# Attention followed by a feed-forward layer: the later q, k, v loads issued by GpSimd instead of SyncE

## The chip, the core and the metric

The program runs on one core of one Trainium2 chip. Its engines work at the same time, each through its own list of instructions in order: TensorE (PE; matmuls, with their weight loads shown apart as PEld), VectorE (DVE), ScalarE (ACT), GpSimd (POOL) and SyncE (SP, which here issues transfers and computes nothing). They meet through semaphores. Sixteen DMA engines move data between the main memory (HBM) and the core's memory (SBUF); a transfer is started by an instruction on the queue of SP, ACT or POOL. TensorE writes its sums to PSUM banks, which VectorE and ScalarE empty. The metric is the time of one execution in microseconds, as the device has it; the medians of several runs are compared.

## The reference

A linear attention with cosine weights, then a two-layer network over all tokens (batch 8, 8 heads, 576 tokens, 64 per head; 512 to 2048 to 512):

```python
def phi(x, c, s):
    r = np.maximum(x, 0.0)
    return np.concatenate([r * c, r * s], axis=-1)
q_p = phi(q, cos_w, sin_w)
k_p = phi(k, cos_w, sin_w)
kv = np.einsum('bhsf,bhsd->bhfd', k_p, v)
z = np.sum(k_p, axis=2)
num = np.einsum('bhsf,bhfd->bhsd', q_p, kv)
den = np.einsum('bhsf,bhf->bhs', q_p, z)[..., None] + 1e-06
attn = num / den
...
h = x @ w_in
g = np.maximum(0.01 * h, h)
return (g @ w_out).astype(np.float32)
```

`x` is the attention's output with the heads of a token side by side, 4608 x 512. Inputs and output are fp32; the kernel computes in fp16 with fp32 sums.

## The kernel before, in words

The kernel goes through the 8 batches b = 0 to 7, and a ninth group, g = 8, takes the last 64 tokens of all batches together. A batch's first 512 tokens are its main part, the other 64 its tail.

For each batch, three fp32 main tiles of 1 MB arrive (q, k, v; `load_main`, L88 to L96), laid out as 128 partitions x 8 heads x 4 tokens x 64, so that each partition takes eight runs of 1 KB from HBM: 1024 runs a tile. The tails of k and v (`load_kvtail`, L98 to L104) are 64 x 4 runs of 256 B in each of two transfers; the tails of q of all batches come late, in eight transfers of 64 x 8 runs of 256 B (`load_qtail`, L106 to L113).

Main tiles share three buffers ("stage", L84 to L86, with two of the w_out tiles and the q tails) and the k and v tails share three others ("kvtail"). A load can start when the last reader of its buffer is done.

The readers are on VectorE and ScalarE. `q_part` and `k_part` take one quarter of a tile at a time and write relu(x) times the cosine or sine to fp16 (L240 on VectorE, L238 on ScalarE); `v_main` converts v to fp16 (L248 on VectorE, L246 on ScalarE). TensorE then forms kv (L289, L298), q is transposed by a DMA from SBUF to SBUF (L346), TensorE forms the numerators and denominators (`num`, L380), VectorE divides (L391 to L396), the result xs is transposed by DMA again (L357), and the two layers follow: `p1` (L785) for the first, `p2` (L890) for the second. From batch 2 on both use Strassen-like sums of quarter matrices, so that VectorE and ScalarE have sums (L251, L254), copies (L795, L805, L908) and the leaky relu (L798, L812) to do beside the loads' conversions. Results leave by `o_store` (L915).

Everything is put in an order written out by hand: each step has a position in one list (`put(position, function, ...)`), the list is sorted by position, and the instructions come out in this order on each engine. The positions of the loads of batches 3 and up are the entries `'load'` of the table `AT`; with them SP's order from batch 3 on is q, k, k tails, v, v tails (batch 3), v, v tails, k, k tails, q (batch 4), then q, k, k tails, v, v tails for each of 5, 6 and 7, with the DMA transposes and the stores in between. Batches 0 to 2 and the weights are loaded by explicit calls earlier. All of these loads are issued by SP in the kernel before. GpSimd makes constants at the start and converts some of w_in and v (L248); its last work is at 46.58 us.

Of the kernel before, what the change touches and what calls it, by code (L numbers as in the profile page):

```python
# [13 lines left out]
P = 128  # L14
# [4 lines left out]
def kernel(  # L19
# [14 lines left out]
    nc = tc.nc  # L34
# [49 lines left out]
    def staged(shape, name, soon=False):  # L84
        p, tag = (early, "early") if soon else (stage, "stage")
        return p.tile(shape, dt.float32, name=name, tag=tag)  # L86

    def load_main(nm, src, b, parts=(0, 1), soon=False):  # L88

        if parts[0] == 0:  # L90
            st[nm, b] = staged([P, H, J, D], f"{nm}st", soon)
        lo, hi = 4 * parts[0], 4 * parts[-1] + 4
        nc.sync.dma_start(
            st[nm, b][:, lo:hi],
            src[b, lo:hi, 0:MAIN, :].rearrange("h (p j) d -> p h j d", j=J),
        )  # L96

    def load_kvtail(nm, src, b):  # L98

        t = kvtail.tile([P, H // 2, D], dt.float32, name=f"{nm}tl", tag="kvtail")  # L100
        v4 = src[b, :, MAIN:S, :].rearrange("(c o) p d -> o p c d", o=2)
        for o in range(2):
            nc.sync.dma_start(t[o:P:2], v4[o])
        st[nm + "t", b] = t  # L104

    def load_qtail(i):  # L106
        if i == 0:
            st["qt"] = staged([P, J, H, D], "qtl")
        for o in range(2):
            nc.sync.dma_start(  # L110
                st["qt"][o * TAIL : (o + 1) * TAIL, i],
                q[2 * i + o, :, MAIN:S, :].rearrange("h p d -> p h d"),
            )  # L113

    def load_k(b):
        load_main("k", k, b)
        load_kvtail("k", k, b)

    def load_v(b):
        load_main("v", v, b)  # L120
        load_kvtail("v", v, b)
# [20 lines left out]
    def load_w2(i):  # L142
        t = staged([P, 4, DM], "w2st", i > 1)
        nc.sync.dma_start(t, w2v[i])
        st["w2", i] = t

    load_main("q", q, 0, (0,))
    load_main("q", q, 0, (1,))
    load_main("k", k, 0, (0,))
    load_main("v", v, 0, (0,))  # L150
    load_kvtail("k", k, 0)
    load_kvtail("v", v, 0)
    load_main("k", k, 0, (1,))
# [943 lines left out]
    for b in range(2, NG):  # L1097
        at_, eng, s0 = AT[min(b, 5)], ENG[min(b, 5)], top[b] if b > 3 else 0
        if b < B:
            for n, pos_ in enumerate(at_.get("load", ())):  # L1100
                put(s0 + pos_, loads, b, n)
            put(s0 + min(at_["kc"] + at_["ks"]) - 0.01, kp_tiles, b)
            for j in range(J + 1):
                put(s0 + at_["kc"][j], k_part, b, j, 0, eng["kc"][j])
                put(s0 + at_["ks"][j], k_part, b, j, 1, eng["ks"][j])
            for n in range(3):
                put(s0 + at_["v"][n], v_part, b, n, eng["v"][n])
            put(s0 + at_["kv"][0], kv_all, b)
        else:
            for j in range(J):  # L1110
                put(s0 - 100 + 3 * j, load_qtail, j)
        for j in range(J):
            put(s0 + at_["qc"][j], q_part, b, j, 0, eng["qc"][j])
            put(s0 + at_["qs"][j], q_part, b, j, 1, eng["qs"][j])
            put(s0 + at_["qt"][j], q_transpose_dma, b, j)
            put(s0 + at_["num"][j], num, b, j)
            put(s0 + at_["xt"][j], x_transpose if b == 2 else x_transpose_dma, b, j)
            put(s0 + at_["xs"][j], x_sums, b, j + 1)
# [33 lines left out]
```

## Time and profile before

| | us |
|---|---|
| median of 3 runs | 272.52 |
| lowest, highest | 271.55, 272.92 |
| the profiled execution, its own time | 273.88 |
| its span, first to last instruction | 272.0 |
| TensorE, VectorE, ScalarE, GpSimd busy in the span | 264.6, 201.0, 200.7, 10.1 |

The page of the profile also shows the DMA queues (share is that of the time of 16 engines):

```profile
q1 hardware_dynamic: 86816, 56.37, 78.1%
q8 instruction: 21, 0.34, 0.5%
```

q1 is SP's queue with its packets, megabytes and share.

How to read the rows. A row of the timeline has the start and the length in us, the engine, the line of the kernel, the operation, what it writes `<-` what it reads, and the shapes; `xN` means N of a kind merged, and brackets hold the idle time before it and what ended that. SPq is SP's queue: the length of a `DMA_DIRECT2D` row there is the time in which SP issues the transfer, not the transfer's own. "To landing" is the time from the start of the issue to the arrival. The chain of waits goes back from the last instruction, at each step to what released it. A row of a sum by stretch has the stretch, its length, and for each engine the busy time with the number of instructions (PE, PEld, DVE, ACT, POOL), the granted clock of TensorE, the DMA engines' share and GB/s. Tile names: `qst`, `kst`, `vst` are the main tiles of q, k and v, `ktl`, `vtl`, `qtl` the tails.

### The profile page before, as it was taken

To read this page: it belongs to the slowest core of one execution; us is meant where nothing else is said; L and a number is where in the kernel's file an instruction comes from. 1 tells how busy PE (TensorE), PEld (TensorE's weight loads), DVE (VectorE), ACT (ScalarE), POOL (GpSimd) and SP (SyncE) were. 2 spreads that over 40 slices of the span, in tenths; PEclk is the share of its full clock that TensorE was granted. 3 is DMA by queue.
4 is the path that set the end of the run, shared out by engine and by line. 5 is a ranking of instruction groups with operands and counts; after the bars stand their busy time and mean duration, and the time that the engine had idled before them with its cause. 6 is when DMAs were issued, how large, how long until landed. Compare 5 with 4: busy or idle time off the path is not lost.

```text
span 272.0 us, 6597 instructions
## 1 busy us (share of the span) xinstructions
PE 264.6 (97%) x2660; PEld 226.8 (83%) x2660; DVE 201.0 (74%) x444; ACT 200.7 (74%) x331; POOL 10.1 (4%) x21
## 2 busy tenths in 40 slices
PE   8999999999999999999999999999999999999994
PEld 5876555665898979889999999999999989999983
DVE  5774589797986797899779696978577757645652
ACT  6756556696878898798899789978966657766621
POOL 1055101000000000000000000000000000000000
PEclk9999999999999999999999999999999999999999
DMA  6999989998999959997999699967274312200314
GB/s 228 318 374 413 398 291 361 368 267 254 309 208 342 175 178 264 312 172 228 259 280 161 183 276 275 181 212 155 62 149 144 61 41 96 80 0 2 154 39 118
DMA packets 87150, 57.05 MB, mean 210 GB/s; under 512 B 56656, under 2 KB 82256, under 8 KB 86608
## 3 DMA queue, kind: packets, MB, share of 16 engines
q1 hardware_dynamic: 86816, 56.37, 78.1%
q8 instruction: 21, 0.34, 0.5%
q10 hardware_dynamic: 304, 0.26, 0.4%
q14 instruction: 9, 0.07, 0.1%
HBM read 36.70 MB, written 9.44 MB: 170 GB/s over the span
## 4 chain that ended last, share of the span: by engine, by line
PE 69%; DMA 3%; DVE 2%; ACT 2%; issue 1%; ACTq 0%; DVEq 0%
PE ps_o L890 31%; PE ps_h L785 27%; PE ps_h L495 3%; DMA qst<-in_q_dram 3%; PE ps_h L890 3%; PE ps_num L380 2%; PE ps_kv L289 2%; DVE gs L254 1%; PE ps_kv L298 0%; ACT g L798 0%; PE ps_xt L445 0%; ACT g L812 0%; DVE xw L254 0%; ACT qp L238 0%; DVE xs L396 0%
## 5 line engine op out<-in xcount | busy, mean ns | idle before, releaser
L890 PEld LDWEIGHTS <-g 128*128 128x128 f16 x640 | 62.5, 98 | 7.3 <-DVE g L251 0.2
L251 DVE TENSOR_TENSOR u<-ps_h,u 128x512 f32<-128x512 f32 x52 | 35.8, 688 | 25.7 <-PE ps_h L785 22.9
L890 PE MATMUL ps_o<-w,g 128*128 128x256 f16 x352 | 51.2, 273 | 0.0
L785 PEld LDWEIGHTS <-w 128*128 128x128 f16 x416 | 44.5, 114 | 1.2
L785 PE MATMUL ps_h<-xT,w 128*128 128x256 f16 x288 | 43.3, 273 | 0.0
L785 PEld LDWEIGHTS <-wa 128*128 128x128 f16 x312 | 34.0, 113 | 2.0 <-DVE xw L254 0.9
L812 ACT ACTIVATE g<-u 128x1024 f16<-128x1024 f32 x26 | 27.5, 1058 | 10.9 <-DVE u L251 10.8
L798 ACT ACTIVATE g<-ps_h 128x512 f16<-128x512 f32 x52 | 31.2, 602 | 5.7 <-PE ps_h L785 5.7
L805 ACT COPY u<-ps_h 128x512 f32<-128x512 f32 x52 | 30.4, 585 | 5.4 <-PE ps_h L785 5.4
L890 PE MATMUL ps_o<-wb,g 128*128 128x256 f16 x232 | 33.5, 273 | 0.0
L785 PE MATMUL ps_h<-xw,wa 128*128 128x256 f16 x208 | 31.3, 273 | 0.6 <-DVE xw L254 0.6
L890 PEld LDWEIGHTS <-gs 128*128 128x128 f16 x256 | 24.9, 98 | 2.9
L908 ACT COPY ob<-ps_o 128x512 f32<-128x512 f32 (+1 forms) x32 | 17.9, 561 | 9.2 <-PE ps_o L890 9.0
L495 PE MATMUL ps_h<-xT,w 128*128 128x512 f16 (+1 forms) x104 | 24.7, 363 | 0.0
L396 DVE TENSOR_TENSOR xs<-ps_num,rden 128x512 f16<-128x512 f32 x28 | 19.4, 691 | 1.0
L890 PE MATMUL ps_o<-w,gs 128*128 128x256 f16 x120 | 17.8, 273 | 0.0
L251 DVE TENSOR_TENSOR ob<-ps_o,ob 128x512 f32<-128x512 f32 (+1 forms) x22 | 14.9, 675 | 3.7 <-ACT ob L908 1.4
L890 PE MATMUL ps_o<-wb,gs 128*128 128x256 f16 x120 | 17.5, 273 | 0.0
L254 DVE TENSOR_TENSOR gs<-g 128x1024 f16<-128x1024 f16 x16 | 11.0, 689 | 8.3 <-ACT g L812 8.1
L795 ACT COPY ps_h<-ps_h 128x512 f32<-128x512 f32 x26 | 14.9, 572 | 2.0 <-PE ps_h L785 1.1
L785 PE MATMUL ps_h<-xw,w 128*128 128x256 f16 x104 | 15.6, 273 | 0.0
L785 PE MATMUL ps_h<-xT,wa 128*128 128x256 f16 x104 | 15.6, 273 | 0.0
(113 smaller groups left out, 408.6 us busy)
## 6 DMA issues: line engine op xcount, KB each, us to landing
qst<-in_q_dram SPq DMA_DIRECT2D x7, 1024.0 KB, 7.0
out_dram<-ob SPq DMA_DIRECT2D x14, 512.0 KB, 2.8
kst<-in_k_dram SPq DMA_DIRECT2D x6, 1024.0 KB, 8.3
vst<-in_v_dram SPq DMA_DIRECT2D x6, 1024.0 KB, 7.1
w1st<-in_moe_w_in_dram SPq DMA_DIRECT2D x8, 512.0 KB, 9.4
w2st<-in_moe_w_out_dram SPq DMA_DIRECT2D x4, 1024.0 KB, 13.8
kst<-in_k_dram SPq DMA_DIRECT2D x4, 512.0 KB, 7.5
vst<-in_v_dram SPq DMA_DIRECT2D x4, 512.0 KB, 7.8
```

Of the source, the lines that this page charges most:

```text
L251: nc.vector.tensor_tensor(out=o, in0=a, in1=b, op=ALU.add)
L254: nc.vector.tensor_tensor(out=o, in0=a, in1=b, op=ALU.subtract)
L289: nc.tensor.matmul(ps[:, n * NE : (n + 1) * NE - 1], lhsT=kpm[:, h, j, :], rhs=vmain[:, h, j, 0 : NE - 1], start=(n == 0 and j == 0), stop ...
L396: nc.vector.tensor_tensor(out=xs, in0=ps[:, :, 0 : 4 * NE].rearrange("p a (b e) -> p a b e", e=NE)[:, :, :, 0:D], in1=rden.rearrange("p (a ...
L495: nc.tensor.matmul(ps[:, lo:hi], lhsT=w1[m // 4][c // 2][:, c % 2, m % 4 : 512 : 4], rhs=st["xT", g][:, c, lo:hi], start=(c == 0 and lo == 0),
L785: nc.tensor.matmul(bank[:, p], lhsT=w(c), rhs=st["xb", g][n][:, c], start=(fresh and p == 0 and c == 0), stop=(c == 1), skip_group_check=True,
L795: nc.scalar.copy(bank1[bj], bank1[bi])
L798: nc.scalar.activation(st["g" + nm, g][:, 2 * t : 2 * t + 2], bank1[bi], AF.Lrelu)
L805: nc.scalar.copy(st["u", g, t][:, n], bank1[bi])
L812: nc.scalar.activation(st["gt", g][:, :, 1, 2 * t : 2 * t + 2], st["u", g, t], AF.Lrelu)
L890: nc.tensor.matmul(bank, lhsT=st[G2[n], g][:, m, pair * P : (pair + 1) * P], rhs=W2[n](m), start=(fresh and m == 0), stop=(m == NH - 1), s ...
L908: nc.scalar.copy(o_at(g, half_, col, pair), bank_of(bi, pair, pair is None))
```

## The change

The loads of q, k and v of batches 3 to 7 (the fourth batch on) are issued on GpSimd's queue, and so are the tails of q. The transfers' shapes, their types, their order among themselves and their places in the list stay; so do the loads of batches 0 to 2 and of the weights, the DMA transposes and the stores, all on SP.

```diff
+    def loader(b):
+        return nc.sync if b < 3 else nc.gpsimd
+
     def load_main(nm, src, b, parts=(0, 1), soon=False):
 
         if parts[0] == 0:
             st[nm, b] = staged([P, H, J, D], f"{nm}st", soon)
         lo, hi = 4 * parts[0], 4 * parts[-1] + 4
-        nc.sync.dma_start(
+        loader(b).dma_start(
             st[nm, b][:, lo:hi],
             src[b, lo:hi, 0:MAIN, :].rearrange("h (p j) d -> p h j d", j=J),
         )
@@
         for o in range(2):
-            nc.sync.dma_start(t[o:P:2], v4[o])
+            loader(b).dma_start(t[o:P:2], v4[o])
         st[nm + "t", b] = t
 
     def load_qtail(i):
         if i == 0:
             st["qt"] = staged([P, J, H, D], "qtl")
         for o in range(2):
-            nc.sync.dma_start(
+            nc.gpsimd.dma_start(
                 st["qt"][o * TAIL : (o + 1) * TAIL, i],
                 q[2 * i + o, :, MAIN:S, :].rearrange("h p d -> p h d"),
             )
```

## The prediction

> **What bounds the kernel now.** I read the page's engine table and its chain first, to see who sets the end.
>
> ```profile
> PE 264.6 (97%) x2660; PEld 226.8 (83%) x2660; DVE 201.0 (74%) x444; ACT 200.7 (74%) x331; POOL 10.1 (4%) x21
> PE 69%; DMA 3%; DVE 2%; ACT 2%; issue 1%; ACTq 0%; DVEq 0%
> ```
>
> TensorE is busy 97% of the span, and the chain runs through it. A modelled busy time can hide slack, so next comes the sum by stretch (columns: length, then the busy time of each engine with its instructions).
>
> ```profile
> 62.00:98.00 36.00, 35.12 (x354) 29.02 (x351) 29.05 (x68) 29.27 (x49) 0.00 (x0) 1.00 1.10 261
> 98.00:190.00 92.00, 91.83 (x1003) 85.67 (x1004) 76.53 (x164) 79.83 (x137) 0.00 (x0) 1.00 0.97 223
> 190.00:262.00 72.00, 72.00 (x719) 67.06 (x717) 46.52 (x86) 48.87 (x82) 0.00 (x0) 1.00 0.29 77
> ```
>
> From 62 us on, where the moved loads are issued and used, TensorE is idle 0.88 + 0.17 + 0 = 1.05 us before the tail, at full granted clock. So there is at most 1.05 us to win, 0.4%. There is much more to lose, because VectorE and ScalarE, which empty TensorE's banks, are themselves busy 81 to 87% of 62 to 190 us, and each works in its own order: one of them that waits for a load holds up everything behind it. VectorE's waits for loads in 62 to 190 us are these (total, times, longest):
>
> ```profile
> DVE qp L240 <- DMA qst<-in_q_dram: 0.7, 1, 0.7
> DVE kpm L240 <- DMA kst<-in_k_dram: 0.6, 1, 0.6
> ```
>
> They are short, but they show that some loads land just when they are needed. The chain of waits passes through one, batch 4's q:
>
> ```profile
> 84.31 8.12 DMA qst<-in_q_dram
> ...
> 98.17 0.63 PE ps_h L785 x4
> ```
>
> That load sets when VectorE and ScalarE go on, and the piece that they hand to TensorE at 98.17 is late by it. A microsecond more on this load is a microsecond more on the end.
>
> **The change part by part.** Every load of batches 3 to 7 leaves SyncE's queue for GpSimd's: 15 main loads of 1 MB (1024 pieces of 1 KB), 20 tails of 64 KB (256 pieces of 256 B) and 8 q tails of 128 KB (512 pieces). Bytes, tiles and readers stay. Three things follow.
>
> *First, what SyncE no longer holds back.* SyncE's queue around batches 3 and 4 (start, length):
>
> ```profile
> 61.74 0.54 SPq L93 DMA_DIRECT2D qst<-in_q_dram  x1
> 62.33 0.56 SPq L93 DMA_DIRECT2D kst<-in_k_dram  x1
> 66.09 0.55 SPq L93 DMA_DIRECT2D vst<-in_v_dram  x1
> 71.12 6.82 SPq L346 DMA_TRANSPOSE qpT<-qp  x4
> 77.98 0.59 SPq L93 DMA_DIRECT2D vst<-in_v_dram  x1
> 80.05 0.54 SPq L93 DMA_DIRECT2D kst<-in_k_dram  x1
> 80.63 3.58 SPq L103 DMA_DIRECT2D ktl<-in_k_dram  x2
> 84.31 0.55 SPq L93 DMA_DIRECT2D qst<-in_q_dram  x1
> ```
>
> Loads stand behind transposes here (v of batch 4 behind 6.82 us of them). On GpSimd a load waits only for its staging buffer and for the loads ahead of it. The buffers are three; the last reads that free them, and the first reads of what lands, are on VectorE
>
> ```profile
> 57.78 0.69 DVE L248 CAST vmain<-vst 128x1024 f16<-128x1024 f32 x1
> 71.47 0.48 DVE L240 TENSOR_SCALAR kpm<-kst,sin_t 128x512 f16<-128x512 f32 x1
> 74.38 0.48 DVE L240 TENSOR_SCALAR qp<-qst,sin_t 128x512 f16<-128x512 f32 x1
> 92.53 0.49 DVE L240 TENSOR_SCALAR qp<-qst,cos_t 128x512 f16<-128x512 f32 x1 [0.75 <-DMA qst<-in_q_dram]
> ```
>
> and on ScalarE
>
> ```profile
> 67.79 0.72 ACT L238 ACTIVATE qp<-qst,cos_t 128x512 f16<-128x512 f32 x1
> 77.95 1.05 ACT L246 CAST vmain<-vst 128x1024 f16<-128x1024 f32 x1
> 78.90 0.73 ACT L238 ACTIVATE kpm<-kst,sin_t 128x512 f16<-128x512 f32 x1
> 89.32 0.73 ACT L238 ACTIVATE kpm<-kst,cos_t 128x512 f16<-128x512 f32 x1 [0.33 <-DMA kst<-in_k_dram]
> ```
>
> So batch 3's first buffer is free at 58.5 (end of the 57.78 row) instead of an issue at 61.74, a lead of 3.2 us; batch 4's v can go at 74.9 instead of 77.98 (3.1); its k at 79.6 instead of 80.05 (0.4); its q's buffer is free at 79.0, so q follows k's tails directly. What SyncE gains (transposes and stores no longer queue behind loads) I price at nothing: TensorE waits 0.17 us in 98 to 190 us, so nothing earlier can be used. The transposes also no longer share one queue with the loads: they may land sooner and the loads later. I price that at nothing too, within 1 us either way.
>
> *Second, what GpSimd's own issue costs.* No run here has a load on GpSimd; the engine's last work is this:
>
> ```profile
> 24.74 1.34 POOL L248 CAST w<-w1st 128x1024 f16<-128x1024 f32 x1 [0.28 <-DMA w1st<-in_moe_w_in_dram]
> 46.58 1.04 POOL L248 CAST vmain<-vst 128x1024 f16<-128x1024 f32 x1 [18.15 <-DMA vst<-in_v_dram]
> ```
>
> After 47.6 it is idle, so nothing else is queued behind its waits. Near bound: it issues like SyncE, 0.55 us a main load. Far bound: it works out the 1024 pieces one after the other; its casts take 1.04 us for 1024 elements a partition, 1.0 ns a step, and with eight steps a piece a main load takes 8.3 us. I choose three steps (source, target, length): 3.1 us a main load, 0.8 a tail, 1.6 a q tail, an estimate, nearer SyncE's row than the far end because the pieces are regular. [...]
>
> Now the ends of issue, with 3.1, 0.8 and these buffer times. Batch 3: q 61.6, k 64.7, two tails 66.3, v 69.4, tails 71.0. SyncE ended them at 62.28, 62.89 and 66.64: q is 0.7 earlier, k 1.8 later, v 2.8 later. The first reads are at 67.79 (q), 71.47 (k) and 77.95 (v), and the page gives k's landing:
>
> ```profile
> kst<-in_k_dram SPq DMA_DIRECT2D x6, 1024.0 KB, 8.3
> ```
>
> 8.3 us from an issue at 62.33 puts k at 70.6, with 0.9 us of slack, so k comes some 0.9 late; v, at 66.09 + 8.3 = 74.4, has 3.5 us and isn't late. Batch 4: v 78.0, tails 79.6, k 82.7, tails 84.3, q 87.4. SyncE ended k at 80.59 and q at 84.86. So k is 2.1 later and q 2.5 later, and both had no slack at all (the reads at 89.32 and 92.53 waited for them). These overlap on the same two engines, so the stage pays the larger: **2.5 us**.
>
> Later batches, in the same way (SyncE, then ScalarE, then landing times of q in 95 to 272 us):
>
> ```profile
> 124.95 0.37 SPq L93 DMA_DIRECT2D qst<-in_q_dram  x1
> ...
> 151.66 0.37 SPq L93 DMA_DIRECT2D qst<-in_q_dram  x1
> 156.06 0.90 SPq L93 DMA_DIRECT2D kst<-in_k_dram  x1
> ```
> ```profile
> 150.58 1.06 ACT L246 CAST vmain<-vst 128x1024 f16<-128x1024 f32 x1
> 160.55 0.71 ACT L238 ACTIVATE qp<-qst,sin_t 128x512 f16<-128x512 f32 x1
> ```
> ```profile
> DMA to landing us min/median/max: 5.6/6.2/7.0
> ```
>
> k waits behind other work on SyncE until 156.06 while its buffer is free at 151.6; on GpSimd q ends at 154.7 and k at 157.8, against 156.96: 0.8 later. q had no lead (issued when its buffer was free) and 160.55 − 151.66 − 7.0 = 1.9 us of slack; it ends 3.1 − 0.4 = 2.7 later, so 0.8 late. With batch 3's k (0.9) that is 1.7 us of lateness at places where other work waits on the two engines; I count a third, **0.5 us**. The q tails, 8 × 1.6 = 13 us from 178 us, come before a stretch in which TensorE has 72.00 of 72.00 us of work; nothing.
>
> *Third, the port.* GpSimd and VectorE get in each other's way in this trace:
>
> ```profile
> 25.22 1.41 DVE L254 TENSOR_TENSOR wa<-wa,w 128x1024 f16<-128x1024 f16 x1
> 26.66 0.69 DVE L254 TENSOR_TENSOR wa<-w,wa 128x1024 f16<-128x1024 f16 x1
> ```
>
> VectorE's subtraction took 1.41 us beside GpSimd's cast of 24.74 to 26.08 and ended 0.55 after it, the same form took 0.69 us alone; the cast took 1.34 instead of 1.04. Whether issuing loads does this is not shown: from nothing to the whole of the rival below. I take **0.5 us**.
>
> Sum: 2.5 + 0.5 + 0.5 = 3.5 us. On the profiled execution (273.88 us, of which 272.0 are its span) that is 277.4; that execution lies 1.36 us over the median of the runs, so against 272.52 the forecast is **276.0 us**. Bounds: at 0.55 us an issue every lead is a gain and the most is −1.05 (271.5); at five steps (5.1 and 1.3) all six main loads and eight tails run back to back and batch 4's q ends at 58.5 + 6 × 5.1 + 8 × 1.3 = 99.5, 14.6 later than 84.86: 287. At four steps (4.1 and 1.0) it is 58.5 + 24.6 + 8 = 91.1, 6.2 later: 279 to 280; at two, q is level and k 1.1 later: 274.
>
> **The rivals.** *Cheap issue.* GpSimd issues in about 1 us. Then only leads remain: batch 4's q ends at 82 (k from 79.6, then two tails and q at 0.25 and 1), 2.8 us earlier, and the 0.75 us wait goes, while 98 to 262 us cannot shrink. Gain 0 to 1.05: 271.5 to 272.8, no slower than before. For it: nothing else is on GpSimd. Against: 1024 pieces in each load.
>
> *The port is held.* While GpSimd writes a load's pieces VectorE's conversions from the staged tiles (L240 and L248) cannot start.
>
> ```profile
> 62.00:190.00 128.00, 22.01 (x50) 1.00 1.01 234
> 62.00:190.00 128.00, 4.11 (x6) 0.00 (x0) 1.00 1.01 234
> ```
>
> These are 26.1 us of 128 on VectorE, 56 operations. 15 main loads × 3.1 us that each block one such operation half the time for half an issue make 15 × 0.5 × 1.5 = 11 us of stalls; VectorE has 128 − 105.6 = 22 us idle there, half of the stalls come out at TensorE: 6 more, 282. Held the other way, GpSimd writes 20% longer (26.1 of 128): 0.6 us a load, 277.5. [...] The rows at 24.74 and 25.22 agree that the two block each other (1.41 for 0.69 us); for loads no run shows it.
>
> *Slow issue.* At 8.3 us a main load and 2.1 a tail a batch costs 3 × 8.3 + 4 × 2.1 = 33 us of GpSimd, more than the 26.7 us between two q loads (124.95 to 151.66 in the queue); then GpSimd is the bound: 5 × 33 = 167 us from 58.5 end at 225:
>
> ```profile
> 174.32 0.69 DVE L248 CAST vmain<-vst 128x1024 f16<-128x1024 f32 x1
> ```
>
> Here VectorE reads batch 7's v, at 174: some 50 us late, 320. At five steps it is the 287 of above. For it: the pieces are short. Against: 8.3 us is eight steps a piece.
>
> **How the numbers follow.** Forecast case (two to four steps, 273.9 to 280): 0.42. Cheap issue: 0.30, of which 0.05 for a median under 271.2 (the spread of the runs helps) and 0.25 for no change. Port held: 0.14 (280 to 286). Slow issue: 0.14 (284 up). Range: 271.4 leaves out 0.05 below; above I cut at 288, which leaves out most of the slow case, 0.11. The forecast's own range is 273.9 to 280. A measurement here tells about 0.5% (1.4 us) from no change: faster 0.05, same 0.25, slower 0.70.
>
> **What would show it.** Right: load issues on GpSimd of 2 to 4 us each; waits of VectorE or ScalarE for qst or kst near 89 to 97 us of 2 us or more; TensorE's busy time in 62 to 98 us short by about 3.5; few waits after 100. Cheap issue: batch 4's q landing before 92.4 and no such wait. Port held: L240 rows longer than 0.48 us, or 22 us of L240 in 62 to 190 grown. Slow issue: v and k later from batch to batch, and waits for vst. I am wrong if TensorE's idle time after 62 us stays near 1 us, or if it grows where no load is waited for.

## The result and the profile after

The changed kernel takes **290.62 us** (median of four runs, 285.52 to 292.98) against 272.05 us (median of four, 271.55 to 272.92) for the kernel before on the same chip. The ratio is 1.057, with a 95% interval of 1.051 to 1.063; it leaves out runs more than 1.5% above the fastest of their kernel, two of the four here, and so lies below the quotient of the medians, 1.068. The profiled execution is the longest of the four, 292.98 us, with a span of 291.2 us: 19.2 us more than the span of 272.0 before. The forecast was 276.0 us with a range up to 288.0: the direction was right, and the loss is four to five times the one forecast (3.5 us), by the ratio or by the medians.

In the changed kernel all lines from L93 on stand three lower (L93 is L96, L346 is L349, L380 is L383, L785 is L788). First the page of the profile after: busy time, the chain of waits by engine, and the DMA queues (packets, MB, share of 16 engines).

```profile
PE 268.5 (92%) x2660; PEld 227.7 (78%) x2660; DVE 202.3 (69%) x444; ACT 200.4 (69%) x331; POOL 42.6 (15%) x64
...
q1 hardware_dynamic: 61552, 38.28, 50.9%
q0 software_dynamic: 5104, 18.09, 22.8%
...
PE 71%; DMA 20%; SPq 3%; issue 2%; DVE 2%; ACT 1%; POOL 0%; DVEq 0%; POOLq 0%
```

The chain of waits now has DMA for 20% of the span, where it had 3%. Of the bytes, 18.09 MB went to a second queue, in packets of 4096 B for the most part (4416 of the 5104 in the trace); SyncE's queue is left with the rest. Now the sum by stretch, over the same stretches as in the prediction (busy us with instructions of PE, PEld, DVE, ACT, POOL, then TensorE's granted clock, DMA share, GB/s).

```profile
62.00:98.00 36.00, 29.09 (x274) 22.56 (x274) 21.29 (x51) 20.68 (x34) 7.41 (x11) 0.86 0.78 222
98.00:190.00 92.00, 83.79 (x873) 75.73 (x872) 67.92 (x147) 71.52 (x123) 15.87 (x21) 0.96 0.93 201
190.00:262.00 72.00, 72.00 (x754) 67.38 (x753) 51.91 (x102) 54.11 (x90) 5.67 (x8) 1.00 0.47 108
```

TensorE is idle 6.91 + 8.21 + 0 = 15.12 us in 62 to 262, where it was idle 1.05: 14.07 us more. The clock has fallen too. The same view cut finer shows where both happen:

```profile
66.00:73.00 7.00, 0.55 (x6) 0.26 (x6) 0.67 (x2) 2.34 (x4) 0.00 (x0) 0.69 1.06 320
73.00:78.00 5.00, 5.00 (x24) 2.61 (x25) 3.45 (x8) 0.95 (x2) 0.00 (x0) 0.50 0.20 73
78.00:98.00 20.00, 20.00 (x211) 17.49 (x210) 14.76 (x35) 15.52 (x28) 5.26 (x7) 0.98 0.80 222
98.00:120.00 22.00, 21.73 (x229) 19.35 (x228) 19.14 (x42) 19.20 (x34) 5.43 (x7) 1.00 0.90 163
120.00:127.00 7.00, 1.05 (x13) 0.71 (x12) 0.83 (x2) 1.12 (x3) 0.00 (x0) 0.73 0.97 219
127.00:130.00 3.00, 3.00 (x12) 1.52 (x11) 1.72 (x5) 0.41 (x1) 0.00 (x0) 0.50 1.14 317
...
180.00:188.00 8.00, 6.01 (x63) 5.15 (x61) 4.10 (x9) 7.97 (x14) 2.13 (x3) 1.00 1.21 238
```

There are two long stalls, at 66 (6.45 us idle) and at 120 (5.95), and a short one at 180 (1.99). Between them TensorE is full. Behind each long stall it works for some microseconds at a clock of 0.50, where a 128x512 matmul of L498 takes 616 to 634 ns instead of 379. By the clock a busy 5.00 us there does the work of 2.5, an estimate: 2.5 + 0.4 + 1.5 = 4.4 us more are lost in 73 to 78, 78 to 98 and 127 to 130. Idle time and half clock together make 14.07 + 4.4 = 18.5 of the 19.2 us.

What TensorE's matmuls wait for (total, times, longest):

```profile
PE ps_num L383 <- DMA qpT<-qp: 13.1, 3, 6.5
```

It is not a load. It is `qpT`, q's transpose by a DMA from SBUF to SBUF, which SyncE still issues as before. Its issue is not late; its landing is. For the last two transposes of batch 2's q, issued between 58.4 and 61, after and then before, the tile's view gives the issue (duration in ns, first and last start) and the time to landing:

```profile
L349 SPq DMA_TRANSPOSE qpT<-qp x2: 1247/1254/1260, 58.4 to 59.7; - x2
...
DMA to landing us min/median/max: 2.9/8.1/13.2
```
```profile
L346 SPq DMA_TRANSPOSE qpT<-qp x2: 1247/1247/1247, 59.0 to 60.4; - x2
...
DMA to landing us min/median/max: 2.8/2.8/2.8
```

The one issued at 59.7 took 13.2 us instead of 2.8 and landed at 72.9, where the first stall ends. In the kernel before, the same transpose landed at 63.2 and TensorE used it at 66.98, a reserve of 3.8 us. What changed beside it is on GpSimd's timeline:

```profile
58.88 1.03 POOL L96 DMA_DIRECT2D qst<-in_q_dram  x1 [12.37 <-DVE kpt L243]
59.91 0.89 POOL L96 DMA_DIRECT2D kst<-in_k_dram  x1
60.79 1.24 POOL L106 DMA_DIRECT2D ktl<-in_k_dram  x2
62.02 0.89 POOL L96 DMA_DIRECT2D vst<-in_v_dram  x1
62.91 1.24 POOL L106 DMA_DIRECT2D vtl<-in_v_dram  x2
```

GpSimd issues a main load in 0.89 us, so that all 3 MB of batch 3 are under way by 64.2. In the kernel before they stood behind the two transposes in one queue. Now they are in another queue, beside the second of them. The DMA queues in 67 to 72, after and then before:

```profile
q0 software_dynamic: 410, 1.52, 92.5%
q1 hardware_dynamic: 412, 0.10, 10.5%
```
```profile
q1 hardware_dynamic: 2270, 1.87, 110.0%
```

410 packets of the one queue and 412 of the other: in these 5 us the counts are those of two queues that are served in turn, one packet each. But a packet of the loads is 4096 B and one of the transpose 256 B, so the loads get 92.5% of the engines' time and the transpose 10.5%. That the engines serve the two in turn is read from these counts alone (220 to 225 in 67 to 70, 190 to 187 in 70 to 72).

Equal turns are not the whole delay. In 61 to 65 the loads already run and the same transpose hardly moves:

```profile
q0 software_dynamic: 172, 0.70, 83.5%
q1 hardware_dynamic: 78, 0.02, 3.9%
```

Of its 1024 packets (256 KB in pieces of 256 B) most go only after 65: in 65 to 67 the counts are 119 of the loads' queue and 540 of the other. Why the first 4 us belong to the loads and the next 2 to the transpose is not shown. The second stall also has a part that turns do not explain: in 119 to 122 both queues almost stand still, with 35 and 20 packets and 45 GB/s. That standstill stays open.

### The profile page after: what moved, and what is told of

Same layout as the page of the kernel before. It is cut to its first block, busy times and chain, and to the rows that moved or that the text cites. A ratio compares the mean times of both kernels' runs of the same rounds, so it can differ in the third digit from the quotient of the medians.

```text
span 291.2 us, 6626 instructions
## 1 busy us (share of the span) xinstructions
PE 268.5 (92%) x2660; PEld 227.7 (78%) x2660; DVE 202.3 (69%) x444; ACT 200.4 (69%) x331; POOL 42.6 (15%) x64
## 3 DMA queue, kind: packets, MB, share of 16 engines
q0 software_dynamic: 5104, 18.09, 22.8%
## 4 chain that ended last, share of the span: by engine, by line
PE 71%; DMA 20%; SPq 3%; issue 2%; DVE 2%; ACT 1%; POOL 0%; DVEq 0%; POOLq 0%
PE ps_o L893 25%; PE ps_h L788 22%; DMA qpT<-qp 12%; PE ps_h L498 6%; PE ps_h L462 5%; PE ps_o L478 5%; DMA qst<-in_q_dram 4%; PE ps_h L893 3%; DMA w1st<-in_moe_w_in_dram 3%; PE ps_num L383 2%; SPq L96 2%; PE ps_kv L292 1%; DMA xT<-xs 1%; SPq L106 1%; PE ps_qt L368 1%
## 5 line engine op out<-in xcount | busy, mean ns | idle before, releaser
L893 PEld LDWEIGHTS <-g 128*128 128x128 f16 x640 | 63.4, 99 | 8.5 <-issue 0.8
L893 PE MATMUL ps_o<-w,g 128*128 128x256 f16 x352 | 52.0, 276 | 0.0
L788 PEld LDWEIGHTS <-w 128*128 128x128 f16 x416 | 44.5, 114 | 2.6 <-issue 1.3
L788 PE MATMUL ps_h<-xT,w 128*128 128x256 f16 x288 | 43.3, 273 | 0.0
L788 PEld LDWEIGHTS <-wa 128*128 128x128 f16 x312 | 34.0, 113 | 1.9 <-DVE xw L257 0.6
L815 ACT ACTIVATE g<-u 128x1024 f16<-128x1024 f32 x26 | 27.5, 1057 | 10.9 <-DVE u L254 10.8
L893 PE MATMUL ps_o<-wb,g 128*128 128x256 f16 x232 | 34.3, 277 | 0.0
L788 PE MATMUL ps_h<-xw,wa 128*128 128x256 f16 x208 | 31.3, 273 | 0.3 <-DVE xw L257 0.3
L498 PE MATMUL ps_h<-xT,w 128*128 128x512 f16 (+1 forms) x104 | 27.3, 392 | 0.0
L383 PE MATMUL ps_num<-kv,qpT 128*128 128x65 f16 (+1 forms) x256 | 12.2, 198 | 13.6 <-DMA qpT<-qp 13.1
L383 PEld LDWEIGHTS <-qpT 128*128 128x128 f16 (+1 forms) x256 | 10.6, 103 | 17.1 <-DMA qpT<-qp 13.9
L394 DVE TENSOR_SCALAR den<-ps_num 128x8 f32<-128x8 f32 x28 | 4.6, 164 | 20.0 <-PE ps_num L383 19.8
## 6 DMA issues: line engine op xcount, KB each, us to landing
kst<-in_k_dram POOLq DMA_DIRECT2D x5, 1024.0 KB, 12.8
```

What stands on the lines that cost most here:

```text
L383: nc.tensor.matmul(ps[lo:hi, h // 4, (h % 4) * NE : (h % 4 + 1) * NE - 1], lhsT=qpT[:, h, lo:hi], rhs=kv[b][:, h, 0 : NE - 1],)
L498: nc.tensor.matmul(ps[:, lo:hi], lhsT=w1[m // 4][c // 2][:, c % 2, m % 4 : 512 : 4], rhs=st["xT", g][:, c, lo:hi], start=(c == 0 and lo == 0),
L788: nc.tensor.matmul(bank[:, p], lhsT=w(c), rhs=st["xb", g][n][:, c], start=(fresh and p == 0 and c == 0), stop=(c == 1), skip_group_check=True,
L815: nc.scalar.activation(st["gt", g][:, :, 1, 2 * t : 2 * t + 2], st["u", g, t], AF.Lrelu)
L893: nc.tensor.matmul(bank, lhsT=st[G2[n], g][:, m, pair * P : (pair + 1) * P], rhs=W2[n](m), start=(fresh and m == 0), stop=(m == NH - 1), s ...
```

## The experiments

**Theory A:** GpSimd's queue stands beside SyncE's; while its loads run, the DMA transposes get only every other packet, TensorE waits for them, and then runs at half clock. **Rival B:** it is the early start of the loads that hurts, on any queue, ScalarE's as well. **Rival C:** GpSimd's issue, or what it holds up on VectorE (the prediction's "port"), is what costs. **Rival D:** any 2 MB at that moment hold a transpose up, in the same queue too. Ratios are to the kernel before, run on the same chip.

**Batch 3 alone, by GpSimd** (`only3_pool`), to see one stall by itself:

```diff
-        return nc.sync if b < 3 else nc.gpsimd
+        return nc.gpsimd if b == 3 else nc.sync
@@ load_qtail
-            nc.gpsimd.dma_start(
+            nc.sync.dma_start(
```

> Only batch 3's loads are on GpSimd, all others on SyncE as before. Theory A (two queues share each DMA engine packet by packet, 4096 B of a load against 256 B of a transpose, so the transpose of batch 2's q that TensorE needs next lands only when the loads are nearly done): the first stall comes back alone, TensorE idle some 6.5 us near 66 us and some 2.5 us of half clock behind it; 272 + 9 = 281 us, no wait for qpT later. Rival C (GpSimd's issuing as such, or the port it shares with VectorE): the loss goes by the number of loads, 3 of 15, so 272 + 19/5 = 276 us without a wait of TensorE for qpT.

Measured: 282.08 us (280.63 to 282.42), ratio 1.035 (1.030 to 1.040). Sum by stretch, then the wait:

```profile
66.00:74.00 8.00, 1.16 (x11) 0.56 (x10) 1.09 (x2) 2.88 (x5) 0.00 (x0) 0.78 1.06 303
74.00:78.00 4.00, 4.00 (x23) 1.90 (x21) 3.45 (x8) 0.30 (x1) 0.00 (x0) 0.58 0.22 79
...
98.00:190.00 92.00, 91.72 (x993) 84.98 (x991) 76.36 (x164) 80.44 (x140) 0.00 (x0) 1.00 0.92 221
```
```profile
PE ps_num L383 <- DMA qpT<-qp: 6.8, 1, 6.8
```

One stall, at the same place, with the same half clock behind it, and from 98 us on only 0.28 us idle. Seven of the 43 loads cost 9.7 of the 18.6 us by the medians, 3.5 of 5.7% by the ratios.

**All but batch 3 by GpSimd** (`from4_pool`), the other half:

```diff
-        return nc.sync if b < 3 else nc.gpsimd
+        return nc.sync if b < 4 else nc.gpsimd
```

> Batch 3's loads are back on SyncE, batches 4 to 7 and the q tails stay on GpSimd. Theory A: the stall near 66 us and its half clock are gone, the later ones (near 120 and 180 us in the changed kernel) stay, some 10 us earlier: 272 + 10 = 280 to 284 us. Rival C: four fifths of the loss, 272 + 15 = 287 us.

Measured: 283.23 us, but the four runs go from 277.40 to 288.27; ratio, formed as above, 1.021 (1.014 to 1.029). In the profiled execution, one of the short ones, the first stall is gone, and `qpT` is waited for once:

```profile
PE ps_num L383 <- DMA qpT<-qp: 2.5, 1, 2.5
```
```profile
111.00:114.00 3.00, 0.53 (x8) 0.25 (x6) 0.72 (x2) 0.95 (x2) 0.00 (x0) 0.92 1.08 296
114.00:118.00 4.00, 4.00 (x27) 2.54 (x25) 1.72 (x5) 0.99 (x2) 0.00 (x0) 0.63 1.12 298
```

By medians the two halves lose 9.7 and 10.9 us, 20.6 together, against 18.6 for the whole; by the ratios 3.5 and 2.1%, against 5.7%. The spread, 10.9 us, leaves the size of this half open, but not its kind.

**The same loads, kept behind the transpose** (`only3_pool_gated`): as `only3_pool`, but GpSimd first copies a column of that transpose's result, so that its loads start when it has landed.

```diff
+    gate = const.tile([P, 1], dt.float16, name="gate")
     def loads(b, which):
+        if b == 3 and which == 0:
+            nc.gpsimd.tensor_copy(gate, st["qpT", 2, 3][:, 0, 0:1])
```

> The same as the kernel with batch 3 alone on GpSimd, but GpSimd first copies one column of batch 2's last transposed q tile, so that its loads start only when that transpose has landed (about 61.2 us instead of 58.9). Theory A: nothing is left to collide with, the stall near 66 us is gone, 272 to 274 us. Rival C: the same loads are issued by the same engine, so the loss of the ungated kernel stays.

Measured: 278.13 us (277.29 to 279.60), ratio 1.021 (1.015 to 1.026). The transpose lands in 3.1 us and TensorE waits for none. But the gate opens at 65.89 and the first load is issued at 66.56, 5.4 us later than expected, and now the load is late. The first reader's wait, then TensorE's:

```profile
ACT qp L241 <- DMA qst<-in_q_dram: 4.5, 2, 3.8
```
```profile
PE ps_o L893 <- ACT xT L449: 3.6, 1, 3.6
```

So the stall on the transpose goes when the loads don't run beside it, as theory A has it. Of the time, 4.0 of the 9.7 us come back: the gate makes a stall of 3.6 us of its own. In the profiled execution, the longest of the four, another 2.4 us are lost in 0 to 30 us, ahead of batch 3's loads (TensorE idle 4.32 us there instead of 1.95); why is not shown.

**ScalarE's queue instead of GpSimd's** (`only3_act`, and `act3_early` with the loads' positions moved forward so that they start with the transpose). Both return `nc.scalar` for batch 3, and the second also has:

```diff
-    3: {'load': (20.5, 24.0, 32.0)
+    3: {'load': (15.0, 15.1, 15.2)
```

> Batch 3's loads on ScalarE's queue: a queue of its own beside SyncE's, but with packets of 1024 B as SyncE's loads have. Theory A: against 1024 B the transpose gets one part in five of the bytes instead of one in seventeen; if loads and transpose meet, the transpose lands 2 to 4 us late instead of 10, and the time is 273 to 277 us. Rival B (the loads merely start 3 us earlier and take the DMA engines, whatever the queue): as bad as on GpSimd, 281 us.

> Batch 3's loads on ScalarE's queue, and earlier in the list, so that they start at about 58 to 60 us as they did on GpSimd and meet batch 2's last transpose. Theory A: load packets of 1024 B, so the transpose's 64 packets an engine let only 1 MB pass (2.7 us): it lands before 67 us; ScalarE's own waits for the buffers cost 1 to 3 us; 273 to 276 us. Rival B (the early start is what hurts, whatever the queue): the transpose lands near 72 us as on GpSimd, TensorE waits some 6 us for qpT, 281 us.

`only3_act`: 273.10 us (272.04 to 277.94), ratio 1.0035 (0.9996 to 1.0073). Its first load was issued at 60.20, when the transposes were all but done (the last landed at 61.47), so it says little on B. `act3_early`: 282.47 us (281.77 to 282.87), ratio 1.038 (1.035 to 1.041), as bad as GpSimd, but for another reason. Its waits, then ScalarE's timeline:

```profile
PE ps_num L383 <- ACT kv L315: 7.8, 1, 7.8
```
```profile
60.18 2.71 ACTq L106 DMA_DIRECT2D ktl<-in_k_dram  x2
62.98 0.77 ACTq L96 DMA_DIRECT2D vst<-in_v_dram  x1
63.80 4.71 ACTq L106 DMA_DIRECT2D vtl<-in_v_dram  x2
68.55 0.59 ACT L315 CAST kv<-ps_kv 128x520 f16<-128x520 f32 x1 [8.05 <-issue]
```

ScalarE spends 60 to 68.5 issuing loads, and the kv that TensorE needs waits behind them. The transpose issued at 59.69 landed 9.8 us later, less than the 13.2 beside GpSimd, more than the 7.3 or less that was expected. The time says nothing on B here, since ScalarE's own stall covers it.

**Only the q loads by GpSimd** (`q_only_pool`): the five main loads of q, 1 MB at a time.

```diff
+        (nc.gpsimd if nm == "q" and b > 2 else nc.sync).dma_start(
```

> Only the five q main loads of batches 3 to 7 are on GpSimd, k, v and all tails on SyncE. Theory A: a transpose is 64 packets on each DMA engine and lets at most as many load packets pass; one main load is 16 packets of 4096 B an engine, so a transpose is held up by at most the time of 1 MB, 2.7 us, less than its slack of some 4 us near 66 us: no wait of TensorE for qpT, 272 to 275 us. Rival C: the loss goes by the number of main loads, a third of 19 us, 278 us.

Measured: 277.55 us (276.22 to 278.81), ratio 1.019 (1.013 to 1.024). This is the number that rival C gave, so the sizes of A were wrong here. But the waits aren't C's:

```profile
PE ps_num L383 <- DMA qpT<-qp: 1.2, 2, 0.9
```
```profile
ACT qp L241 <- DMA qst<-in_q_dram: 4.7, 2, 3.3
```

The transpose of 60.47 landed 8.0 us later, and in the last two batches q itself is late: GpSimd issued it in 0.88 us each time, so the issue is not slow, but beside SyncE's traffic, which is now k, v and the transposes, it took 8.9 and 11.3 us to land, where the kernel before has 6.2 and 7.0. I had counted the packets as if only one side paid. (The 2.7 us for 1 MB was an estimate; the kernel before moves 375 GB/s in 67 to 72, which makes 2.8.)

**The cause by itself** (`extra_pool`, `extra_act`, `extra_sync`). To take the edit, the late loads and the issuing engine's own work out of it, these add to the kernel before two loads of 1 MB that nothing reads, at 199 us, where TensorE has some reserve. The first two put them on GpSimd's and on ScalarE's queue, behind a copy of a column of `xs`; the third on SyncE's own queue, right behind the same two transposes (here without the copy, with `nc.sync`, at the place of the second transpose).

```diff
+    gate = const.tile([P, 1], dt.float16, name="gate")
+    def extra():
+        nc.gpsimd.tensor_copy(gate, st["xs", 7, 4 - 1][:, 0, 0:1])
+        for n in range(2):
+            nc.gpsimd.dma_start(
+                staged([P, H, J, D], f"spare{n}"),
+                (k, v)[n][3, :, 0:MAIN, :].rearrange("h (p j) d -> p h j d", j=J),
+            )
+    put(top[7] - 6.89, extra)
```

> The kernel before with two more loads of 1 MB that nothing reads, issued by GpSimd when batch 7's last xs tile is written (about 197 us), where the DMA engines are nearly idle, just ahead of two transposes of qp that landed 3.9 and 3.5 us after their issue in the kernel before and were read 7 us later. Theory A: 32 load packets of 4096 B an engine pass during the first transpose's 64: both transposes land some 5 us later than before, 8 to 9.5 us after issue; the time is unchanged, 272 to 273 us, because nothing needs them sooner. Rival B and C: a transpose already under way is not held up by loads on another queue: 4 to 5 us.

> The same two loads on ScalarE's queue with the same start. Theory A: 128 packets of 1024 B an engine; the first transpose's 64 packets let 64 pass, 1 MB: it lands 2.7 us later than before, 6 to 7 us after issue, the second some 5 us later, 8 to 9 us; 272 to 274 us. If the size of the packets does not matter, both are as late as with GpSimd's loads.

> The kernel before with two loads of 1 MB that nothing reads, issued by SyncE right behind the two transposes of about 199 us, so in the same queue as they. Theory A (it is the second queue that holds the transposes up; one queue serves in order): the two transposes land as in the kernel before, 3 to 5 us after their issue, although 2 MB are issued within 2 us of them; what is behind the loads lands later, up to 7 us. Rival D (any 2 MB at that time holds them up, whatever queue): they land 9 to 13 us after their issue, as beside the same loads on another queue. Time by A 272 to 274, by D 275 to 276.

The time from issue to landing of the two transposes at about 199 us (201 and 203 in the run with ScalarE's queue), as the tile's view has it (the lower, the middle, the higher of the two): in the kernel before, with the loads on GpSimd's queue, on ScalarE's, and on SyncE's.

```profile
DMA to landing us min/median/max: 3.5/3.7/3.9
```
```profile
DMA to landing us min/median/max: 12.8/13.0/13.3
```
```profile
DMA to landing us min/median/max: 9.4/9.7/10.0
```
```profile
DMA to landing us min/median/max: 4.2/4.3/4.4
```

The same 2 MB make the transposes take 3.5 times as long from GpSimd's queue, 2.6 times from ScalarE's, and 1.2 times from their own. The times are 275.99 us (two runs), ratio 1.015 (1.009 to 1.020); 275.02 (two runs), 1.011 (1.004 to 1.018); 272.78 (nine), 1.0001 (0.998 to 1.002). The first two do not measure the extra loads alone: TensorE waits for a `qpT` only in the first, 0.9 us, and in the profiled executions it is idle 4.31 and 5.69 us in 0 to 190 us, ahead of the extra loads, where the kernel before has 3.35; with ScalarE's loads it is not idle at all in 190 to 262. So it is the landings that test the theory here.

Rival D falls for the kernel with one queue: there the loads went out at 201.6, when the transposes of 197.9 and 199.3 were some 2 us or less from landing, and cost nothing. What 2 MB that move at the very same time in that queue would do, the run doesn't show. What of rival B stands is that ScalarE's queue does it too. Its loads have packets of 1024 B, GpSimd's of 4096 B, which fits the smaller delay; but the two queues may differ in more, so that the packet size decides is argued and not shown. Turns by packets show here too, with ScalarE's loads in 207 to 210:

```profile
q10 hardware_dynamic: 746, 0.76, 82.8%
q1 hardware_dynamic: 741, 0.19, 31.7%
```

(q10 is ScalarE's queue.) And as in the first stall the loads go ahead before that: 817 packets to 14 in 203 to 206. Theory A had the sign of all three and the sizes of `extra_sync`; for the other two its sizes were too small, most of all beside GpSimd.

**Why too little: the loads where nothing else runs** (`extra_quiet`): the same two loads by GpSimd, behind a tile of the last group.

```diff
+        nc.gpsimd.tensor_copy(gate, st["g11", 8][:, 0, 0:1])
...
+    put(top[8] + 20, extra)
```

> The kernel before with the same two unread loads of 1 MB by GpSimd, but behind the gate of a late tile of the last group, where no transpose is in flight. Beside transposes the pair landed 12.5 us after the second issue. If the two queues only alternate, the 2 MB alone take about 6 us (the rate of the main loads on SyncE's queue) and the pair lands 6 to 8 us after its first issue: mixing slows both sides. If GpSimd's packets are slow by themselves: 10 to 13 us here too. Time: 272 to 274.

The two loads, from issue to landing: alone (issued at 237.2 and 238.2), then beside the transposes (198.8 and 199.8).

```profile
DMA to landing us min/median/max: 6.6/7.6/8.5
```
```profile
DMA to landing us min/median/max: 8.9/10.7/12.5
```

Alone the pair is done 8.51 + 1.03 = 9.5 us after its first issue, beside the transposes 13.6: between the two answers that were expected, so both sides pay. The packets themselves last longer when mixed. Means over all packets of the trace, in ns:

```
                          4096 B of GpSimd    256 B of transposes
loads alone  225 to 250        193                  20
before       198 to 205         -                   26
mixed        198 to 213        256                  36
```

The single run took 274.96 us, with TensorE idle after 100 us no longer than before; one run has no interval, and the 2.7 us above the median before are not explained.

**Only the tails by GpSimd** (`tails_pool`): 20 of the 43 moved instructions, but 1.3 of the 18 MB.

```diff
-            loader(b).dma_start(t[o:P:2], v4[o])
+            (nc.gpsimd if b > 2 else nc.sync).dma_start(t[o:P:2], v4[o])
```

> Only the 20 tails of k and v of batches 3 to 7 (64 KB each) are issued by GpSimd; main loads and q tails are SyncE's as in the kernel before. Theory A (packets of a second queue hold the transposes up, in proportion to their bytes): a pair of tails is 128 KB against 2 MB of a pair of main loads, so a transpose beside them is held up by well under 1 us and TensorE never waits: 271.5 to 272.8, no change. Rival C (GpSimd's issue or the port is what costs): 20 of the 43 instructions moved are here, and by count of instructions they carry 43% to 47% of the loss of 18.6 us: 280 to 281.

Measured: 273.74 us (272.33 to 275.33, 12 runs), ratio 1.0048 (1.0023 to 1.0073). Rival C's 280 is out: the count of instructions doesn't carry the loss (20 of 43 cost 1.3 of 18.6 us); the bytes, 1.3 of 18 MB, fit it here. "No change" was not quite right either: 1.3 us slower, and the profile has one wait that the kernel before has not:

```profile
PE ps_o L893 <- ACT xT L449: 1.4, 1, 1.4
```

ScalarE comes late to that step because it waited 1.6 us for batch 3's q. That load, on SyncE, took 7.6 us to land instead of 5.9, with four tails in the other queue.

## Why the prediction was wrong

**The step that failed** is in the first part: "The transposes also no longer share one queue with the loads: they may land sooner and the loads later. I price that at nothing too, within 1 us either way." The sign was backwards and the size wrong by more than ten times. What the runs showed instead: the transpose lands later (13.2 us instead of 2.8), because the order of one queue, transposes first, is gone. Loads on another queue went ahead of it (172 packets to 78) and from 67 on took turns with it by packets (410 to 412), in which the side with the small packets lost (10.5% of the engines' time to 92.5%). This carries the first stall of TensorE, 6.45 us, with the half clock behind it, as `only3_pool` has it alone. The second, 5.95 us, is a wait for the same kind of transpose (14.4 us to landing; the two of batch 4 there took 5.6 and 5.9 before), but the standstill from 119 on that reaches into it is not explained. I had looked for what SyncE's queue holds back, and found loads behind transposes; the order also protected the transposes from the loads. A row of the kind that should have warned me was quoted: 6.82 us of `qpT` issues in the middle of the loads, on the way to `num`. The one that stalled first stood just ahead of the quoted rows, issued at 60.40, with a reserve of 3.8 us.

**What SyncE gains, nothing:** right. After 62 us no stretch has less idle time than before.

**GpSimd's issue** was mis-sized. A main load was put at 3.1 us, a tail at 0.8, a q tail at 1.6. The groups of GpSimd's issues (busy us in all, mean ns of one):

```profile
L106 POOL DMA_DIRECT2D ktl<-in_k_dram x10 | 6.4, 643 | 0.0
...
L113 POOL DMA_DIRECT2D qtl<-in_q_dram x8 | 5.7, 717 | 14.3 <-DVE u L254 14.3
...
L96 POOL DMA_DIRECT2D kst<-in_k_dram x5 | 4.4, 886 | 5.4 <-DVE vmain L251 3.7 <-ACT vmain L249 1.7
```

0.89, 0.64 and 0.72 us: near SyncE's 0.55, far from the far bound of 8.3. That is 0.9 ns a piece (0.89 us / 1024), not three steps of 1 ns. So slow issue falls.

**Batch 4's q, 2.5 us:** not there. TensorE is idle 0.27 us in 78 to 120, where that q is used. It was issued at 90.28; less the 9.4 us already lost by then (6.45 + 2.5 + 0.4) that is 80.9, 3.4 us earlier than the 84.31 of before. The cheap-issue rival had 2.8 earlier. **Later batches' lateness, 0.5 us:** its reason, the slow issue, was wrong; the waits for loads that the last runs show go with longer landings beside the other queue (7.6 us instead of 5.9 in `tails_pool`, 8.9 and 11.3 instead of 6.2 and 7.0 in `q_only_pool`).

**The port, 0.5 us:** the word stands for what the two rows of 25.22 and 26.66 show, 1.41 us of VectorE beside a cast of GpSimd and 0.69 alone; what the two engines share, no run shows. Beside issues, too, some conversions of VectorE took longer, and it doesn't reach the path. Over the whole run, VectorE's conversions of q by the cosine (L243; the same group before was 481 ns on average):

```profile
L243 DVE TENSOR_SCALAR qp<-qst,cos_t 128x512 f16<-128x512 f32 x18 | 9.2, 512 | 1.4 <-DMA qst<-in_q_dram 1.4
```

Four conversions of 481 ns took 562, 633, 689 and 697, and each of them lies beside an issue on GpSimd; that is 0.66 us of VectorE in all. Five others of q beside an issue took 0.47 to 0.48 us, and the other operations of VectorE that overlap one have the times they have alone (0.48 the conversions of k, 0.68 to 0.69 the sums of 128x1024). Issues of main loads on GpSimd ran between 0.88 and 1.19 us. "The port is held", with 6 us or more, falls.

**The cheap-issue rival** had the issue right (0.89 against "about 1 us") and still the wrong end, 271.5 to 272.8 "no slower than before": it rested on the same unpriced step. So did my range's low end. Fast issue may even make it worse, since 3 MB are in the other queue at once; that was not tested.

**What would make it wrong** was named: TensorE's idle time growing "where no load is waited for". That is what happened.

Open: how much of the loss each stall carries from run to run (285.52 to 292.98 for the change, 277.40 to 288.27 for its later half); the 1.99 us at 180, of which 1.2 are a wait for ScalarE; and why `q_only_pool` and `only3_pool_gated` lose more than the waits named above. Part of that lies ahead of every moved load: in 0 to 30 us TensorE is idle 1.95 us in the profile before, 3.19 after, 3.34 in `q_only_pool` and 4.32 in `only3_pool_gated`, and no run says why. Loads and transposes together on GpSimd's queue were not tried. No version that was run is faster than the kernel before.

## What to carry to other kernels

Here the move of the loads to another engine's queue removed the order between them and the transposes left on the old one, and a transpose landed 13.2 us after its issue instead of 2.8. Before such a move, list what short, urgent transfers stand ahead of the loads, and price them as if they shared the DMA engines packet by packet, with their packet size against the load's. That price was too low in both runs made for it: 8 to 9.5 us for `extra_pool`, where 12.8 and 13.3 were measured, and 6 to 9 for `extra_act`, where it was 9.4 and 10.0. If the path waits for such transfers, as here for transposes with packets of 256 B, keep the loads in the same queue behind them (2.8 us to landing in the kernel before, 4.2 and 4.4 in `extra_sync`), or start them when these have landed (3.1 us in `only3_pool_gated`, where the load was then late).

## What the runs showed of the hardware

- Two queues took turns by packets in two stretches: 410 to 412 in 5 us, 1.52 MB to 0.10 MB, with packets of 4096 B against 256 (the changed kernel); 746 to 741 in 3 us, 0.76 MB to 0.19 MB, with 1024 B against 256 (`extra_act`). They didn't do so from the start: before that it was 172 to 78 in 4 us and then 119 to 540 in 2 us, loads to transposes, and in `extra_act` 817 to 14 in 3 us.
- The same load, 1024 runs of 1 KB, travelled as packets of 1024 B from SyncE's and ScalarE's queues and of 4096 B from GpSimd's (means by size in the trace: 46 to 56 and 193 to 256 ns).
- Mixing slowed both sides in `extra_pool`: the pair of loads took 13.6 us instead of 9.5, the transposes 13.0 instead of 3.7.
- The stalls of 6.45 and 5.95 us cost more than their length. By stretches of 1 us, the clock stayed at 0.50 for 5.9 us of work behind the first and 3.7 behind the second, and behind a wait of 2.5 us in `from4_pool` it was 0.63 over 4 us. What sets these times, no run shows.
- Loads that ScalarE issued held ScalarE itself: in `act3_early` its compute stood 8.05 us behind issues that took 2.71 and 4.71 us for a pair of tails, which GpSimd issued in 1.24.
